# The last 64 query rows of a head pair: one unit for both batches, on four 64x64 pieces of TensorE's array

## The chip, the cores and the metric

One core of one Trainium2 chip runs the whole program. The metric is the device time of one execution in microseconds (us), as a median over several runs.

## What is computed

Attention with a learned relative bias over 2 batches, 8 heads, 576 positions and 64 dimensions, then two gated layers over its 1152 tokens (512 to 1536 to 512), the second with a norm ahead of it. The change touches the attention alone:

```python
scores = scale * np.matmul(q, k.transpose(0, 1, 3, 2))
...
scores = scores + bias.transpose(2, 0, 1)[None, :, :, :]
scores = scores - np.max(scores, axis=-1, keepdims=True)
attn = np.exp(scores)
attn = attn / (np.sum(attn, axis=-1, keepdims=True) + 1e-09)
return np.matmul(attn, v).astype(np.float32)
```

The bias depends on head and positions, not on the batch, so both batches use the same bias rows.

## The kernel before

576 query rows are four blocks of 128 and one of 64 (`it` 0 to 4; block 4 is the one of 64). Heads go in pairs (`hp` 0 to 3), since a head has 64 dimensions. A unit is a batch, a head pair and a row block: 40 units, in the order of `UNITS` (L264 to L267). The last eight, 32 to 39, are the 64-row units, for each head pair batch 0 and then batch 1.

A unit goes through these stages, in float32:

- `qk_mm` (L302): scores `s`. The stationary operand is a head's queries, 64 dimensions on the partitions, and the moving one its keys, in two chunks of 288 columns. Head 0 of the pair lies on partitions 0 to 63 of `raw`, head 1 on 64 to 127. With 128 rows each head fills a PSUM tile of two banks; with 64 rows both heads share one tile, head 0 in its partitions 0 to 63 and head 1 in 64 to 127, so that one reduction and one exponential serve both. Such a unit has one "job" where a 128-row unit has two (L298).
- `reduce_min` (VectorE, L322) adds the bias and takes the row's minimum of the negated scores; `expo` (ScalarE, L342) makes the exponentials and their sums; `normal` (L356) divides, on GpSimd but for the first units.
- `transp` (L370) transposes the probabilities in blocks of 128 columns into banks `tp`, up to four blocks a bank: nine blocks for 128 rows, five, the last of 64 columns, for 64 rows. Two or three copies (`evac`, L705 on ScalarE, L703 on VectorE) bring them to `pt`.
- `pv` (L391) multiplies with V: five steps of two matmuls, one per head, on the two column halves of the array. For 64 rows the fifth step has 64 contraction rows. `xf`, `xh`, `xl` are the copy of the result and its split into two parts for the expert layers. V has three parts in memory, `vp`: head 0, head 1 shifted by 64 rows (its first 64 positions lie alone in chunk 0), and head 1 unshifted, which only the 64-row units use and which `load_last` (L146) brings late.

The loop over `n` (L693) runs `qk_mm(n + 1)`, the reductions and exponentials of unit `n`, `normal(n - 1)`, and `transp` and `pv` of unit `n - 3`. The order of these within a pass is written out by hand (`ORDERS`, L58): one string for passes 0 to 19, one for later passes, one for the drain of the last four passes, in which no scores are left. In the drain the first two of a unit's copies go to ScalarE and the third to VectorE; in the passes before it the first goes to ScalarE and the rest to VectorE.

`C` in these strings is `advance`: one micro step of the weights' preparation for the expert layers in a pass (two and more in the drain). A weight piece of 128x512 comes from memory as pairs of words (`wr`) and is split by four micro steps on VectorE, ScalarE and GpSimd (L478 to L496) into a high and a low part, `wh` and `wl`. Behind attention come 72 steps `s` of the expert layers: `gate_val` (products `gv`, L511) and `out_mm` (products `acc`, L541), with five micro steps a step or fewer. The first `gate_val`, `gv0`, stands in the drain of attention. Micro steps go by count and by the number of pieces done, not by time.

The SyncE queue issues the loads, in program order: bias rows `bt` up to four units ahead into three buffers, V's parts, weights two pieces ahead.

## Time and profile before

| | us |
|---|---|
| median of 3 runs | 658.17 |
| lowest, highest | 657.31, 658.32 |
| span of the profiled execution | 654.7 |
| PE busy | 641.9 |
| DVE busy | 486.9 |
| ACT busy | 354.4 |
| POOL busy | 209.6 |

The page gives the profiled execution by its span, from the first to the last instruction; the median lies 3.5 us above it, which is what stands around the span. PE is TensorE, DVE VectorE, ACT ScalarE, POOL GpSimd, SPq the SyncE queue. The attention ends at about 198 us of the span, the rest is the expert layers. The start of an instruction in a timeline row is measured; its length holds its latency, so the time that a block takes on PE is read from its start to the start of the next block.

### The profile page before, as it was taken

The numbers are of one execution on the slowest core, as the hardware profiler recorded it, in microseconds if no ns is written. First come the engines' busy times: TensorE is split into PE (matmuls) and PEld (weight loads), VectorE is DVE, ScalarE is ACT, GpSimd is POOL, SyncE is SP. The second block draws the span as 40 slices with busy tenths as digits, with TensorE's granted clock in tenths as the row PEclk, the third lists the DMA queues.
The fourth block names the chain that finished last, engine by engine and source line by source line (L and its number), as shares of the span: only waits on it lengthen the run. The fifth ranks groups of instructions, "written<-read, shape, count | busy, mean of one in ns | idle before, by whom it ended". The sixth has DMA issues, their size and how long they took to land.

```text
span 654.7 us, 11794 instructions
## 1 busy us (share of the span) xinstructions
PE 641.9 (98%) x4454; PEld 576.1 (88%) x4454; DVE 486.9 (74%) x980; ACT 354.4 (54%) x753; POOL 209.6 (32%) x237
## 2 busy tenths in 40 slices
PE   8889999999999999999999999999999999999997
PEld 4336666777779999999999999999999999999997
DVE  6889898688659987888888888787877878321322
ACT  4769888888786655445444545453545535111110
POOL 6401677566454332333323321110423423000000
PEclk9979999999999999999999999999999999999999
DMA  8875855664124333433332330220324321000111
GB/s 202 278 263 185 223 173 183 220 227 121 52 65 130 111 115 97 129 97 98 102 102 90 127 95 34 65 66 32 102 93 129 97 76 55 2 0 1 49 49 48
DMA packets 28089, 71.73 MB, mean 110 GB/s; under 512 B 3457, under 2 KB 6529, under 8 KB 28033
## 3 DMA queue, kind: packets, MB, share of 16 engines
q1 hardware_dynamic: 27168, 69.80, 34.7%
q10 hardware_dynamic: 864, 1.18, 0.5%
q8 instruction: 35, 0.57, 0.4%
q14 instruction: 22, 0.17, 0.1%
HBM read 57.72 MB, written 13.25 MB: 108 GB/s over the span
## 4 chain that ended last, share of the span: by engine, by line
PE 94%; ACT 1%; issue 0%; DVE 0%; DVEq 0%
PE gv L511 46%; PE s L312 7%; PE pv L404 7%; PE tp L384 6%; PE bps L213 4%; PE acc122a L541 1%; PE acc102b L541 1%; PE acc100b L541 1%; PE acc121b L541 1%; PE acc120b L541 1%; PE acc101b L541 1%; PE acc110b L541 1%; PE acc030b L541 1%; PE acc112b L541 1%; PE acc111b L541 1%; PE acc032b L541 1%
## 5 line engine op out<-in xcount | busy, mean ns | idle before, releaser
L488 POOL TENSOR_TENSOR ff<-ff,wr 128x512 int32<-128x512 int32 x72 | 113.3, 1574 | 250.8 <-DVE ff L487 130.8
L517 DVE TENSOR_TENSOR g<-gv,sg 128x384 f32<-128x384 f32 x72 | 40.0, 556 | 95.6 <-PE gv L511 81.6
L519 ACT ACTIVATE gh<-g 128x384 fp32r<-128x384 f32 x72 | 37.8, 525 | 101.1 <-DVE g L517 101.1
L511 PE MATMUL gv<-nh,wv 128*128 128x384 f32 x288 | 76.5, 337 | 0.0
L511 PE MATMUL gv<-xh,wh 128*128 128x384 f32 x216 | 73.2, 339 | 0.0
L511 PE MATMUL gv<-xl,wh 128*128 128x384 f32 x216 | 72.9, 337 | 0.0
L511 PE MATMUL gv<-xh,wl 128*128 128x384 f32 x216 | 72.8, 337 | 0.0
L478 DVE TENSOR_SCALAR ff<-wr 128x512 uint32<-128x512 uint32 x72 | 62.1, 863 | 0.0
L515 ACT ACTIVATE sg<-gv 128x384 f32<-128x384 f32 x72 | 34.6, 481 | 50.1 <-PE gv L511 50.0
L330 DVE CUSTOM_DVE_ANT_0 t<-s,bt 128x576 f32<-128x576 f32 x72 | 51.8, 751 | 13.4 <-PE s L312 11.3
L312 PE MATMUL s<-raw 64*128 64x288 f32 (+1 forms) x320 | 52.3, 427 | 4.9 <-issue 2.9
L351 ACT ACTIVATE p<-t,mn 128x576 f32<-128x576 f32 x72 | 55.2, 767 | 3.0 <-DVE mn L330 3.0
L404 PEld LDWEIGHTS pv<-pt,v 128*64 128x64 f32 (+1 forms) x800 | 40.2, 136 | 17.2 <-ACT pt L705 11.1
L195 DVE TENSOR_SCALAR ht<-w1l,bpc 128x304 f32<-128x304 f32 (+17 forms) x100 | 53.5, 599 | 0.0
L511 PEld LDWEIGHTS gv<-nh,wv 128*128 128x128 f32 x288 | 52.4, 188 | 0.0
L404 PE MATMUL pv<-pt,v 128*64 128x128 f32 (+2 forms) x800 | 49.6, 268 | 1.4 <-ACT pt L705 1.4
L492 ACT ACTIVATE wh<-ab 128x512 fp32r<-128x512 f32 x42 | 26.4, 630 | 45.2 <-DVE ab L491 44.7
L525 DVE TENSOR_TENSOR gl<-g,gh 128x384 fp32r<-128x384 f32 x72 | 45.3, 629 | 7.0 <-ACT gh L519 7.0
L487 DVE SCALAR_TENSOR_TENSOR ff<-wr,ff 128x512 uint32<-128x512 uint32 x72 | 49.1, 682 | 0.0
L491 DVE SCALAR_TENSOR_TENSOR ab<-ab,ff 128x512 f32<-128x512 f32 x72 | 49.1, 682 | 0.0
L511 PE MATMUL gv<-nh,wh 128*128 128x384 f32 x144 | 48.7, 338 | 0.0
L366 POOL TENSOR_SCALAR p<-p,rs 128x576 f32<-128x576 f32 x60 | 48.2, 815 | 1.4 <-DVE rs L361 1.1
(358 smaller groups left out, 1583.3 us busy)
## 6 DMA issues: line engine op xcount, KB each, us to landing
wr<-wts SPq DMA_DIRECT2D x72, 512.0 KB, 3.6
bias_d<-be SPq DMA_DIRECT2D x36, 295.5 KB, 4.5
bt<-bias_d SPq DMA_DIRECT2D x16, 576.0 KB, 4.8
raw<-qk SPq DMA_DIRECT2D x16, 288.0 KB, 6.5
v<-vp SPq DMA_DIRECT2D x8, 320.0 KB, 4.5
v<-vp SPq DMA_DIRECT2D x8, 160.0 KB, 4.7
bt<-bias_d SPq DMA_DIRECT2D x8, 144.0 KB, 3.3
out<-part SPq DMA_DIRECT2D x6, 192.0 KB, 1.9
```

Source lines behind the costliest of these rows:

```text
L195: nc.vector.tensor_scalar(ht, src, bpc[:, t : t + 1], 0.0, op0=ALU.add, op1=ALU.max)
L312: nc.tensor.matmul(dst, raw[r, 0, it * 128 : it * 128 + rows_of(it)], raw[r, 1, hf * 288 : hf * 288 + 288], start=True, stop=True,)
L330: nc.vector.tensor_tensor_reduce(t, sp[:, :, :288], bt[:, j].rearrange("p (a c) -> p a c", a=2), -SCALE, 3.0e38, ALU.add, ALU.min, mn[:, j ...
L351: nc.scalar.activation(p[:, j], t.rearrange("p a c -> p (a c)"), AF.Exp, bias=mn[:, j : j + 1], scale=-1.0, accum_out=sm[:, j : j + 1],)
L366: nc.gpsimd.tensor_scalar(p[:, j], p[:, j], rs[:, j : j + 1], 1.0, op0=ALU.mult, op1=ALU.mult)
L404: nc.tensor.matmul(box["ps"][j * 64 : j * 64 + 64, :n], v[:k, 2 * j if it == 4 else j, c, :], pt[:k, c, j * 64 : j * 64 + 64] if it == 4 e ...
L478: nc.vector.tensor_scalar(ff, hw, 3, 0x3FFFFFFF, op0=ALU.logical_shift_left, op1=ALU.bitwise_and)
L487: nc.vector.scalar_tensor_tensor(ff, hw, 0xC0000000, ff, op0=ALU.bitwise_and, op1=ALU.bitwise_or)
L488: nc.gpsimd.tensor_tensor(ff.bitcast(I32), ff.bitcast(I32), lw.bitcast(I32), op=ALU.add)
L491: nc.vector.scalar_tensor_tensor(ab, ab, TINY_HI, ff.bitcast(F32), op0=ALU.is_ge, op1=ALU.mult)
L511: nc.tensor.matmul(ps[:, :CH], wt[:, cs], xt[:, cc, :], start=(k == 0), stop=(k == 11))
L541: nc.tensor.matmul(dst, st_[:, m * 128 : m * 128 + 128], mv, start=(head and k == 0), stop=(last and k == 2))
```

## The change

The 64-row units 32 to 39 become four, 32 to 35, one per head pair, with `None` for the batch. Such a unit has two jobs again, one per batch: the score tile `s{n}_0` belongs to batch 0 and `s{n}_1` to batch 1, each with head 0 in partitions 0 to 63 and head 1 in 64 to 127. So that the four products of a chunk (two batches, two heads) lie on four different pieces of the array, batch 1 keeps its heads in the other halves of `raw` (`half`). The probabilities of both batches are one row of 1152 columns and are transposed in nine blocks; block 4 holds the last 64 columns of batch 0 and the first 64 of batch 1. V for batch 1 is therefore taken shifted by 64 rows, and `load_last` puts head 0 shifted into its third part by three DMAs, where batch 0 keeps one. All products have 128 contraction rows; where a block holds columns of the other batch, V's rows are zero. Both batches' products go into one bank, side by side. The loop has 36 passes instead of 40. `BLK`, `groups_of` and `IT_OF` give the same blocks as before, and without `jobs` every unit has two reductions, exponentials and divisions; `place` is the splitting into `xh` and `xl` by itself.

```diff
@@ -129,11 +140,15 @@
 
     raws = {}
 
+    def half(b, h):
+        x = (h + b) % 2 * 64
+        return slice(x, x + 64)
+
     def load_raw(b, hp):
         t = wk.tile([128, 2, S], F32, tag=f"raw{hp // 2}", name=f"raw{b}{hp}", bufs=4)
         raws[b, hp] = t
         for h in range(2):
-            r = slice(h * 64, h * 64 + 64)
+            r = half(b, h)
             nc.sync.dma_start(t[r], qk[b, hp][:, r, h].rearrange("w p s -> p w s"))
 
     vs = {}
@@ -144,7 +159,13 @@
         nc.sync.dma_start(vs[b, hp][:, :2], vp[b, hp][:, :2])
 
     def load_last(b, hp):
-        nc.sync.dma_start(vs[b, hp][:, 2], vp[b, hp][:, 2])
+        v, src = vs[b, hp], vp[b, hp]
+        if b == 0:
+            nc.sync.dma_start(v[:, 2], src[:, 2])
+            return
+        nc.sync.dma_start(v[64:, 2], src[:64, 0])
+        nc.sync.dma_start(v[:64, 2, 1:], src[64:, 0, :4])
+        nc.sync.dma_start(v[:64, 2, 0], src[:64, 1, 0])
 
     def drain(q, k=99):
         while q and k:
@@ -263,65 +285,57 @@
 
     BLOCKS = [(hp, it) for hps in ((0, 1), (2, 3)) for it in ITS[:3] for hp in hps]
     BLOCKS += [(hp, it) for it in ITS[3:] for hp in range(NP)]
-    UNITS = [(b, hp, it) for hp, it in BLOCKS for b in range(B)]
+    UNITS = [(b, hp, it) for hp, it in BLOCKS for b in (range(B) if rows_of(it) == 128 else (None,))]
     NU = len(UNITS)
     st = {}
 
     def load_bias(n):
-        _, hp, it = UNITS[n]
+        b, hp, it = UNITS[n]
         bt = wk.tile([128, 2, S], F32, tag="bt", name=f"bt{n}", bufs=3)
 
...
-        st[n, "bt"] = st[n + 1, "bt"] = bt
-
-    ahead = list(range(0, NU, B))
+        st[n, "bt"] = bt
+        if b is not None:
+            st[n + 1, "bt"] = bt
+
+    ahead = [n for n in range(NU) if UNITS[n][0] != 1]
...
     def qk_mm(n):
         b, hp, it = UNITS[n]
-        raw = raws[b, hp]
-        sps = [bank2(f"s{n}_{j}") for j in range(jobs(n))]
-        if it == 4:
-            order = [(h, hf, sps[0][h * 64 : h * 64 + 64, hf, :288]) for h in range(2) for hf in range(2)]
+        sps = [bank2(f"s{n}_{j}") for j in range(2)]
+        if b is None:
+            plan = [(x, h, sps[x][h * 64 : h * 64 + 64]) for x in range(2) for h in range(2)]
         else:
-            order = [(h, hf, sps[h][:, hf, :288]) for hf in range(2) for h in range(2)]
-        for h, hf, dst in order:
-            r = slice(h * 64, h * 64 + 64)
-            nc.tensor.matmul(
-                dst,
-                raw[r, 0, it * 128 : it * 128 + rows_of(it)],
-                raw[r, 1, hf * 288 : hf * 288 + 288],
-                start=True,
-                stop=True,
-            )
+            plan = [(b, h, sps[h]) for h in range(2)]
+        r0, rows = BLK[it]
+        for hf in range(2):
+            cs = slice(hf * 288, hf * 288 + 288)
+            for x, h, dst in plan:
+                raw, r = raws[x, hp], half(x, h)
+                nc.tensor.matmul(dst[:, hf, :288], raw[r, 0, r0 : r0 + rows], raw[r, 1, cs], start=True, stop=True)
         for j, sp in enumerate(sps):
             st[n, "s", j] = sp
 
     def reduce_min(n, j):
-        if j >= jobs(n):
-            return
         if j == 0:
             st[n, "mn"] = w2.tile([128, 2], F32, tag="mn", name=f"mn{n}", bufs=3)
         bt, mn = st[n, "bt"], st[n, "mn"]
@@ -368,66 +379,70 @@
     pts = {}
 
     def transp(n):
-        b, hp, it = UNITS[n]
-        pt = pts[b, hp, it] = w2.tile([128, 9, 128], F32, tag="pt", name=f"pt{n}")
-        p = st.pop((n, "p"))[0]
-        p2 = p.rearrange("p a c -> p (a c)")
-        width = S if it == 4 else 2 * S
-        blocks = [p2[:, a : min(a + 128, width)] for a in range(0, width, 128)]
+        pt = pts[UNITS[n]] = w2.tile([128, 9, 128], F32, tag="pt", name=f"pt{n}")
+        p = st.pop((n, "p"))[0].rearrange("p a c -> p (a c)")
         evac = []
-        i = 0
-        while i < len(blocks):
-            m = min(4, len(blocks) - i)
+        for i in range(0, 9, 4):
+            m = min(4, 9 - i)
             tp = bank(f"tp{n}_{i}")
             for x in range(m):
-                k = blocks[i + x].shape[1]
-                nc.tensor.transpose(tp[:k, x * 128 : x * 128 + 128], blocks[i + x], ident)
-            evac.append((pt[:k, i : i + m], tp[:k, : m * 128].rearrange("p (m c) -> p m c", m=m)))
-            i += m
+                a = (i + x) * 128
+                nc.tensor.transpose(tp[:, x * 128 : x * 128 + 128], p[:, a : a + 128], ident)
+            evac.append((pt[:, i : i + m], tp[:, : m * 128].rearrange("p (m c) -> p m c", m=m)))
         return evac
 
     peq = []
...
     def pv(u):
         b, hp, it = u
         pt = pts.pop(u)
-        v = vs[b, hp]
-        n = rows_of(it)
+        r0, n = BLK[it]
         box = {}
-
-        def step(c):
+        if b is None:
+            todo = [(x, c, j) for x in range(B) for c in range(5) for j in range(2)]
+        else:
+            todo = [(b, c, j) for c in range(5) for j in range(2)]
+        k = len(todo) // 5
+
+        def one(x, c, j):
+            v = vs[x, hp]
+            if b is None:
+                at, w, m = x * 64, (2 * j if x == 0 else 2 - j), pt[:, 4 * x + c, j * 64 : j * 64 + 64]
+            else:
+                at, w, m = 0, j, pt[:, 4 * j + c]
+            dst = box["ps"][j * 64 : j * 64 + 64, at : at + n]
+            nc.tensor.matmul(dst, v[:, w, c, :], m, start=(c == 0), stop=(c == 4))
+
+        def step(i):
             def go():
-                if c == 0:
+                if i == 0:
                     box["ps"] = bank(f"pv{b}{hp}{it}")
-                for j in range(2):
-                    k = 64 if it == 4 and c == 4 else 128
-                    nc.tensor.matmul(
-                        box["ps"][j * 64 : j * 64 + 64, :n],
-                        v[:k, 2 * j if it == 4 else j, c, :],
-                        pt[:k, c, j * 64 : j * 64 + 64] if it == 4 else pt[:, j * 4 + c, :n],
-                        start=(c == 0),
-                        stop=(c == 4),
-                    )
-                if c < 4:
+                for t in todo[i * k : i * k + k]:
+                    one(*t)
+                if i < 4:
                     return
...
                 xf = w2.tile([128, 128], F32, tag="xf", name=f"xf{b}{hp}{it}")
...
+                if b is None:
+                    for x in range(B):
+                        place(xf[:, x * 64 : x * 64 + 64], x, hp, x * S + r0, n)
+                else:
+                    place(xf, b, hp, b * S + r0, n)
```

On PE, in the passes of the 64-row units: `s36` is the scores of unit 36, `tp34` the transposes of unit 34, `pv104` the products of batch 1, head pair 0, block 4. Before:

```order
L312 MATMUL s36_0_2643<-raw02_856 64x288 x4
L404 MATMUL pv133_2654<-pt31_2583,v13_1540 64x128 x10
L384 MATMUL tp33_0_2681<-ident_94,p33_2530 128x128 x4
L384 MATMUL tp33_4_2686<-ident_94,p33_2530 64x128
L312 MATMUL s37_0_2688<-raw12_912 64x288 x4
L404 MATMUL pv004_2699<-pt32_2635,v00_519 64x64 x10
L384 MATMUL tp34_0_2723<-ident_94,p34_2578 128x128 x4
L384 MATMUL tp34_4_2728<-ident_94,p34_2578 64x128
L312 MATMUL s38_0_2730<-raw03_966 64x288 x4
L404 MATMUL pv104_2741<-pt33_2680,v10_587 64x64 x10
```

and now, from the scores of the last unit, 35:

```order
L334 MATMUL s35_0_2631<-raw03_966 64x288 x2
L334 MATMUL s35_1_2632<-raw13_1039 64x288 x2
L334 MATMUL s35_0_2631<-raw03_966 64x288 x2
L334 MATMUL s35_1_2632<-raw13_1039 64x288 x2
L425 MATMUL pv033_2650<-pt30_2561,v03_1464 64x128 x10
L390 MATMUL tp32_0_2677<-ident_94,p32_2496 128x128 x4
L390 MATMUL tp32_4_2682<-ident_94,p32_2496 128x128 x4
L390 MATMUL tp32_8_2687<-ident_94,p32_2496 128x128
L425 MATMUL pv133_2698<-pt31_2618,v13_1540 64x128 x10
```

Four score matmuls in one row have become eight, which change between the batches' tiles, and the transposes of a 64-row unit are the nine of a 128-row unit.

On PE in the drain, behind `gv0`, before:

```order
L384 MATMUL tp38_0_2925<-ident_94,p38_2759 128x128 x4
L384 MATMUL tp38_4_2930<-ident_94,p38_2759 64x128
L404 MATMUL pv124_2942<-pt37_2854,v12_1392 64x64 x10
L384 MATMUL tp39_0_2960<-ident_94,p39_2801 128x128 x4
L384 MATMUL tp39_4_2965<-ident_94,p39_2801 64x128
L404 MATMUL pv034_2974<-pt38_2924,v03_1464 64x64 x10
L404 MATMUL pv134_2998<-pt39_2959,v13_1540 64x64 x10
```

and now:

```order
L390 MATMUL tp34_0_2821<-ident_94,p34_2613 128x128 x4
L390 MATMUL tp34_4_2826<-ident_94,p34_2613 128x128 x4
L390 MATMUL tp34_8_2831<-ident_94,p34_2613 128x128
L425 MATMUL pvNone14_2844<-pt33_2731,v01_661 64x64 x10
L425 MATMUL pvNone14_2844<-pt33_2731,v11_733 64x64 x10
L390 MATMUL tp35_0_2874<-ident_94,p35_2670 128x128 x4
L390 MATMUL tp35_4_2879<-ident_94,p35_2670 128x128 x4
L390 MATMUL tp35_8_2884<-ident_94,p35_2670 128x128
L425 MATMUL pvNone24_2894<-pt34_2820,v02_1322 64x64 x10
L425 MATMUL pvNone24_2894<-pt34_2820,v12_1392 64x64 x10
L425 MATMUL pvNone34_2930<-pt35_2873,v03_1464 64x64 x10
L425 MATMUL pvNone34_2930<-pt35_2873,v13_1540 64x64 x10
```

The same four blocks of products and transposes in turn, each for two batches: the transposes of two units and the products of three.

On ACT in the drain, behind the copy `gh` of the first expert step, where `pt` are the copies of transposed blocks and `ab`, `wr`, `wh` micro steps of weights. Before:

```order
L519 ACTIVATE gh0_2922<-g32_0_2920 128x384
L705 ACTIVATE pt38_2924<-tp38_0_2925 128x512
L480 ACTIVATE ab6_2938<-wr6_2632 128x512
L481 ACTIVATE wr6_2632<-wr6_2632 128x512
L705 ACTIVATE pt38_2924<-tp38_4_2930 64x128
L416 ACTIVATE xf124_2953<-pv124_2942 128x64
L422 ACTIVATE xh2_119<-xf124_2953 128x64
L492 ACTIVATE wh5_1792<-ab5_2869 128x512
L705 ACTIVATE pt39_2959<-tp39_0_2960 128x512
L705 ACTIVATE pt39_2959<-tp39_4_2965 64x128
```

and now:

```order
L534 ACTIVATE gh0_2818<-g32_0_2816 128x384
L720 ACTIVATE pt34_2820<-tp34_0_2821 128x512
L495 ACTIVATE ab5_2840<-wr5_2438 128x512
L496 ACTIVATE wr5_2438<-wr5_2438 128x512
L720 ACTIVATE pt34_2820<-tp34_4_2826 128x512
L436 ACTIVATE xfNone14_2865<-pvNone14_2844 128x128
L403 ACTIVATE xh1_118<-xfNone14_2865 128x64
L403 ACTIVATE xh2_119<-xfNone14_2865 128x64
L507 ACTIVATE wh4_1790<-ab4_2753 128x512
L720 ACTIVATE pt35_2873<-tp35_0_2874 128x512
L720 ACTIVATE pt35_2873<-tp35_4_2879 128x512
```

The second copy of a unit has grown from 64x128 to 128x512 and stands, as before, behind two micro steps; the pieces that are being prepared at this place are one number lower.

## Rows read from the trace of the kernel before

**Rows 1.** The page: span, and PE's busy time with its share and instructions.
```profile
span 654.7 us, 11794 instructions
PE 641.9 (98%) x4454; PEld 576.1 (88%) x4454; DVE 486.9 (74%) x980; ACT 354.4 (54%) x753; POOL 209.6 (32%) x237
```
**Rows 2.** Stretches: length, then busy time (instructions) of each engine, PEclk, DMA share, GB/s.
```profile
60.00:160.00 100.00, 100.00 (x1060) 71.39 (x1054) 83.16 (x230) 85.90 (x218) 64.21 (x102) 1.00 0.63 191
157.53:161.08 3.55, 3.55 (x39) 2.73 (x38) 3.18 (x9) 2.59 (x8) 3.16 (x5) 1.00 0.23 81
161.08:164.58 3.50, 3.50 (x39) 2.53 (x38) 2.55 (x10) 2.59 (x8) 1.93 (x4) 1.00 0.50 159
172.70:198.00 25.30, 23.92 (x299) 18.25 (x297) 15.46 (x41) 19.81 (x52) 13.26 (x20) 1.00 0.21 64
198.00:300.00 102.00, 102.00 (x586) 101.84 (x584) 89.82 (x139) 54.88 (x106) 34.93 (x23) 1.00 0.37 114
```
**Rows 3.** Timeline of PE: start, length, instruction, [idle before <-releaser].
```profile
158.70 1.31 PE L404 MATMUL pv<-pt,v 128*64 128x128 f32 x20
159.94 1.20 PE L384 MATMUL tp<-ident,p 128*128 128x128 f32 x9
161.08 1.19 PE L312 MATMUL s<-raw 64*64 64x288 f32 x8
...
179.71 0.77 PE L384 MATMUL tp<-ident,p 128*128 128x128 f32 x5
180.40 1.20 PE L312 MATMUL s<-raw 64*64 64x288 f32 x8
181.52 0.95 PE L404 MATMUL pv<-pt,v 128*64 128x64 f32 x20
182.40 0.77 PE L384 MATMUL tp<-ident,p 128*128 128x128 f32 x5
...
192.51 0.71 PE L384 MATMUL tp<-ident,p 128*128 128x128 f32 x5
...
195.72 0.95 PE L404 MATMUL pv<-pt,v 128*64 128x64 f32 x20 [0.93 <-ACT pt L705]
197.11 0.95 PE L404 MATMUL pv<-pt,v 128*64 128x64 f32 x20 [0.45 <-ACT pt L705]
197.99 0.45 PE L511 MATMUL gv<-xh,wh 128*128 128x384 f32 x1
```
**Rows 4.** Timeline of PE in slices: 180.39 to 180.45, to 180.75, 157.52 to .55, 178.82 to .86, 107.04 to .08.
```profile
180.40 0.47 PE L312 MATMUL s<-raw 64*64 64x288 f32 x2
180.40 0.71 PE L312 MATMUL s<-raw 64*64 64x288 f32 x4
157.53 0.51 PE L312 MATMUL s<-raw 64*128 64x288 f32 x2
178.83 0.28 PE L404 MATMUL pv<-pt,v 128*64 128x64 f32 x2
107.05 0.44 PE L213 MATMUL bps<-ht,prms 128*32 128x272 f32 x4
```
**Rows 5.** Timeline of PE in two slices, 178.92 to 178.95 and 178.92 to 179.30.
```profile
178.83 0.34 PE L404 MATMUL pv<-pt,v 128*64 128x64 f32 x4
178.83 0.69 PE L404 MATMUL pv<-pt,v 128*64 128x64 f32 x16
```
**Rows 6.** Timeline of ACT in the drain of attention.
```profile
193.80 0.58 ACT L705 ACTIVATE pt<-tp 128x512 f32<-128x512 f32 x1
194.28 0.67 ACT L480 ACTIVATE ab<-wr 128x512 f32<-128x512 f32 x1
194.85 0.66 ACT L481 ACTIVATE wr<-wr 128x512 int32<-128x512 uint32 x1
```
**Rows 7.** Timeline of the SyncE queue: issuing V's third parts of two units.
```profile
147.26 1.06 SPq L147 DMA_DIRECT2D v<-vp  x2
```
**Rows 8.** The page's groups: one of DVE's four steps on a weight piece.
```profile
L487 DVE SCALAR_TENSOR_TENSOR ff<-wr,ff 128x512 uint32<-128x512 uint32 x72 | 49.1, 682 | 0.0
```

More of the change, by code (lines that the diff above doesn't have):

```diff
@@ L64, with groups_of @@
 TINY_HI = 1.125 * 2.0**-15
+BLK = ((0, 128), (128, 128), (256, 128), (384, 128), (512, 64))
 def rows_of(it):
-    return 128 if it < 4 else 64
+    return BLK[it][1]
+def groups_of(it):
+    a, r = BLK[it]
+    return range(a // 16, (a + r) // 16)
+IT_OF = {T: it for it in range(5) for T in groups_of(it)}
 def bias_width(it):
@@ L239, in bias_end @@
             nc.gpsimd.tensor_scalar(dst, src, 1.0, 1.0, op0=ALU.mult, op1=ALU.mult)
-        a = (T // 8) * 128 + rows_of(T // 8) - 1 - right
-        r = (T % 8) * 128
-        nc.sync.dma_start(bias_d[T // 8][r : r + 128, a : a + S + 15], be)
+        it = IT_OF[T]
+        a = sum(BLK[it]) - 1 - right
+        r = (T - groups_of(it)[0]) * 128
+        nc.sync.dma_start(bias_d[it][r : r + 128, a : a + S + 15], be)
         stored.append(T)
-    GORDER = [T for it in ITS for T in range(8 * it, min(8 * it + 8, 36))]
+    GORDER = [T for it in ITS for T in groups_of(it)]
     GORDER = GORDER[2:8] + GORDER[:2] + GORDER[8:]
@@ L276, in load_bias @@
         flat = bias_d[it].rearrange("a w -> (a w)")
-        for h in range(2 if it == 4 else 1):
+        for h in range(2 if b is None else 1):
             o = r - 1 + (2 * hp + h) * w
             rows = flat[o : o + r * (H * w - 1)].rearrange("(i k) -> i k", k=H * w - 1)
-            if it == 4:
+            if b is None:
                 nc.sync.dma_start(bt[h * 64 : h * 64 + 64, 0], rows[:, :S])
@@ L332, in reduce_min @@
             sp[:, :, :288],
-            bt[:, j].rearrange("p (a c) -> p a c", a=2),
+            bt[:, 0 if UNITS[n][0] is None else j].rearrange("p (a c) -> p a c", a=2),
             -SCALE,
@@ L357, in normal @@
         p, sm = st[n, "p"]
-        k = jobs(n)
-        nc.vector.tensor_scalar(sm[:, :k], sm[:, :k], 1e-9, None, op0=ALU.add)
+        nc.vector.tensor_scalar(sm, sm, 1e-9, None, op0=ALU.add)
         rs = w2.tile([128, 2], F32, tag="rs", name=f"rs{n}", bufs=3)
-        nc.vector.reciprocal(rs[:, :k], sm[:, :k])
-        for j in range(k):
+        nc.vector.reciprocal(rs, sm)
+        for j in range(2):
             if n in NORM_DVE:
@@ L370, in transp, with place @@
     def transp(n):
-        b, hp, it = UNITS[n]
-        pt = pts[b, hp, it] = w2.tile([128, 9, 128], F32, tag="pt", name=f"pt{n}")
-        p = st.pop((n, "p"))[0]
-        p2 = p.rearrange("p a c -> p (a c)")
-        width = S if it == 4 else 2 * S
-        blocks = [p2[:, a : min(a + 128, width)] for a in range(0, width, 128)]
+        pt = pts[UNITS[n]] = w2.tile([128, 9, 128], F32, tag="pt", name=f"pt{n}")
+        p = st.pop((n, "p"))[0].rearrange("p a c -> p (a c)")
         evac = []
-        i = 0
-        while i < len(blocks):
-            m = min(4, len(blocks) - i)
+        for i in range(0, 9, 4):
+            m = min(4, 9 - i)
             tp = bank(f"tp{n}_{i}")
             for x in range(m):
-                k = blocks[i + x].shape[1]
-                nc.tensor.transpose(tp[:k, x * 128 : x * 128 + 128], blocks[i + x], ident)
-            evac.append((pt[:k, i : i + m], tp[:k, : m * 128].rearrange("p (m c) -> p m c", m=m)))
-            i += m
+                a = (i + x) * 128
+                nc.tensor.transpose(tp[:, x * 128 : x * 128 + 128], p[:, a : a + 128], ident)
+            evac.append((pt[:, i : i + m], tp[:, : m * 128].rearrange("p (m c) -> p m c", m=m)))
         return evac
     peq = []
+    def place(ps, b, hp, lo, n):
+        a = lo
+        while a < lo + n:
+            e = min(lo + n, (a // CH + 1) * CH)
+            d = slice(a % CH, a % CH + e - a)
+            src = ps[:, a - lo : e - lo]
+            nc.scalar.activation(xh[a // CH][:, hp, d], src, AF.Copy)
+            nc.gpsimd.tensor_tensor(xl[a // CH][:, hp, d], src, xh[a // CH][:, hp, d].bitcast(F32), op=ALU.subtract)
+            a = e
     def pv(u):
@@ L428, in step @@
+                if b is None:
+                    for x in range(B):
+                        place(xf[:, x * 64 : x * 64 + 64], x, hp, x * S + r0, n)
+                else:
+                    place(xf, b, hp, b * S + r0, n)
             return go
-        peq.extend(step(c) for c in range(5))
+        peq.extend(step(i) for i in range(5))
     def members(l, g):
```

21 lines of the change are left out of this document (2 added, 19 removed).

## Prediction, made before the changed kernel ran

> **What bounds the kernel now.** I read the page first: TensorE (PE) is busy 98% of the span of 654.7 us [rows 1]. Then the stretches: from 60 to 160 us and from 198 to 300 us PE has no idle time at all, at clock 1.00 (2.4 GHz), while VectorE (DVE), the next busiest, is at 83 to 88%. Only the end of attention, 172.70 to 198.00, has a gap, 23.92 us busy of 25.30 [rows 2]. So in attention a microsecond of PE time is a microsecond of the result, and the expert layers behind it, which start when attention's last product is done, should move as a block. The reader is to see in [rows 3] that PE runs three blocks per loop pass back to back: scores (`s`), products with V (`pv`) of the unit four before, transposes (`tp`) of the unit three before, all as if nothing else existed.
>
> **The cycle of a 64-row unit, before.** Starts in [rows 3]: transposes 179.71 to 180.40, 0.69; scores 180.40 to 181.52, 1.12; products 181.52 to 182.40, 0.88. That is 2.69 us, and eight such units (two batches, four head pairs) exist. A 128-row unit takes 1.14 for its nine transposes (159.94 to 161.08) and 1.24 for its products, and its whole pass lasts 3.55 [rows 2, 3]. The 64-row unit has half the rows and yet costs three quarters.
>
> **Scores: the main term.** The program has four score matmuls per 64-row unit, the trace has eight records (x8), so each float32 matmul is two passes. They start in pairs: in a slice of 0.06 us at 180.40 two stand, and by 180.75 four [rows 4]. A pass of 288 columns thus runs on two pieces of the array at a time, and four starts fill the 1.12 us. The new unit has eight matmuls, sixteen passes, on four pieces: row half x column half. If all four run together, sixteen passes are again four starts and 1.12 us for both batches; the price of the second unit, 1.12, is gone, four times: **4.49 us**. No row shows four pieces of 64x64 at once, so this is the one unknown price. From both sides: four at once gives 4 x 1.12 less; two at once gives no saving; one at a time gives 16 passes of 0.24 us (1.12 less the ends, by four starts), 3.9 us against 2.25, a loss of 1.6 per head pair. I take four, because each kind of neighbour is seen running together: different row halves into different banks (64x128 scores, two records in 0.03 us at 157.53), different column strips on the same rows with different moving data (`pv`, two at 178.83; `bps`, four strips at 107.05), and row half plus column half crossed (64x64 scores) [rows 4].
>
> The first two matmuls of the new order are the two heads of batch 0: different row halves, different column halves, the same bank of scores. In the rows of before the two records that start together at 180.40 must be just that pair, since the two column chunks of one head use the same piece and each head begins with the same chunk, that is the same bank. The Trainium skill says against it ("TensorEngine Tiling (Array Packing)", Restrictions and Gotchas) that different row tiles cannot access the same PSUM bank simultaneously; by that rule at most two pieces would run here, the scores would save nothing, and the sum below would be 3.5 instead of 7.8 us. The paired starts of the 64x64 scores speak against the rule as it is written, at least where the rows go to different partitions of the bank.
>
> **Transposes.** Before, each unit has 576 columns in five blocks, the last of 64; both together ten. Now the 1152 columns of both batches are one row of nine full blocks, and the middle one holds the end of batch 0 and the start of batch 1. 2 x 0.69 becomes 1.14: 0.24 per pair, **1.0 us** in all.
>
> **Products.** The number stays, 20 per head pair, all 64 columns wide, in column pairs. Before, each unit has eight pairs of passes with 128 rows, then two with 64 rows, and the start of a block and the change to 64 rows cost time: 0.88 per unit. Between the end of the second pair and of the eighth lie 0.35 us [rows 5], 0.058 a pair. Twenty pairs without a change of shape: the eighth ends 0.69 after the start, twelve more add 0.70, 1.39; in the 128-row block the next block begins 0.07 before the last end (1.31 long, next start 1.24 later [rows 3]), so 1.32. Against 1.76: 0.44, four times **1.76 us**. The zero rows that V is padded with replace the 64-row passes.
>
> Sum of PE work: 4.49 + 1.0 + 1.76 = **7.25 us**.
>
> **The gap at the end.** Before, PE stands 0.93 and 0.45 us before the last two product blocks, both for ScalarE's (ACT) copies of transposed blocks [rows 3]. In the drain the first expert product `gv0` runs on PE until G = 192.51, and behind it ACT does the copy of 512 columns, two weight steps, the second copy, and so on [rows 3, 6]. Now three whole units are left instead of three half ones: the second copy has 512 columns too, 0.58 long, instead of 128, but PE has 1.32 instead of 0.88 of products per unit as cover. ACT starts the first copy at G+1.29; the copy and the two steps take 0.48 + 0.57 + 0.56 from start to start, then a copy of 0.5, G+3.4. PE does nine transposes and the products of unit 33 until G+2.46, the first four transposes of unit 35 until 2.9, then needs a bank that the second copy frees (four banks go round): 3.45, a stall of 0.5. The products of unit 34 end near 5.5; ACT by then has the output copies (0.6 by my estimate, three of 128 partitions and at most 128 columns), one weight step (0.5) and two copies of 512 (1.0), 5.5 to 5.7: a stall of 0.1 to 0.2. So I take **0.7 of gap instead of 1.38**; ends: none, and 2.5 if one more of ACT's or DVE's steps comes late (0.5 to 0.7 each, two or three of them).
>
> **Costed at nothing.** The second score reduction, exponential and normalization per pass: a merged pass has on DVE, ACT and GpSimd what a 128-row pass has, and there DVE is busy 3.18 of 3.55 us with PE never idle; merged passes have 3.50 on PE (as 161.08 to 164.58, where DVE does 2.55 now) [rows 2]. That cover is thin, 0.3 us: three passes without it would cost 1 us. The eight extra DMAs for V on the SyncE queue: about 0.5 us each to issue (1.06 for two [rows 7]), 4 us spread over eight passes of 3.5, and V's third part is used some 20 us after its load. Bias loads: the same eight transfers, but they now follow a pass apart and wait for one of three buffers, so the queue holds back the weight loads behind it by a pass, 3.5 us; weights are fetched two pieces ahead, some eight passes. The four weight steps that lose their pass: attention has 36 passes instead of 40 and each carries one step, so the pipeline of split weights is one piece behind at the same place in the program. A piece costs DVE four steps of about 0.68, 2.7 us, and from 198 to 300 DVE has 12 us free [rows 2, 8]. The first weights that could be late are piece 4's, for the second half of `gv1`: their last step, `wl4`, follows on DVE the copy of unit 35's last block (near G+4.5) and one weight step, and waits for ACT's `wh4` (near G+4.6), so it ends near G+5.8, while the second half of `gv1` begins 2.1 us after G+7. If that cover fails, a piece is 2.7 us.
>
> **Sum.** 7.25 + 0.7 = 7.95; for four starts instead of two in each round, some 0.02 us, I take off 0.1: **7.8 us**, span 654.7 to 646.9. The runs' median is 658.17, 3.5 us above the profiled span; that stays: **650.4 us**.
>
> **Rivals.**
> *Two pieces at a time* (by the bank or the shared row strip): scores save nothing, 7.95 - 4.49 = 3.5, 654.7 us. For it: no row with four; against: all pairs seen. 9%.
> *The drain or the late weights eat two to three microseconds:* a whole piece, 2.7 us late before `gv1` or the output product, 650.4 + 2.7 = 653.1, or the gap at its upper end, 652.0. For it: ACT already ended both waits [rows 3, 6]. 6%.
> *One piece at a time* (the other side): if a piece must wait for the one before, since consecutive matmuls share alternately bank and rows, a merged unit's scores take 3.9 instead of 2.25 us, 6.6 lost against 3.4 won elsewhere: 661.4. It decides once the scores take over 3.1 us per unit, on average 1.25 pieces at a time. Against it stand the pairs of [rows 4]. 3%.
> *It moves nothing:* the split weights come at a pace of their own, and the expert layers wait for what attention has won, 657.3 to 658.3 as now. For it: the steps are a piece behind; against: from 198 to 300 the DMA engines are at 0.37 of their time and DVE has room [rows 2]. 2%.
>
> **How the numbers follow.** Forecast, four pieces and a short gap: 80%, with 649.5 (no gap) less 0.5 for the spread of runs (657.31 to 658.32) down to 649.0, and 652.0 up with the long gap. The range takes in the late weights with the spread: 649.0 to 653.2, leaving out two at a time, one at a time and no change, 14%. About 0.2%, 1.3 us, is what a measurement tells here from no change. Faster by more: 80 + 9 + 6, less one for cases in between, 94%; within: 2%; slower: 4%.
>
> **What would show it.** Scores of a merged unit: sixteen records, four starting within some 0.05 us, 1.12 to 1.15 us before the next block (2.2 would be two at a time, over 3 one). Nine transposes in 1.14, twenty product pairs in 1.32. `gv1` starts near 190.1 instead of 197.99, with PE waits of 0.2 to 1.2 us for ACT's copies in the drain; behind it PE without gaps, ending the same distance later. I am wrong if a merged pass on PE exceeds 3.6 us, if `gv1` waits for a weight, or if a stretch in the expert layers shows idle PE.

## The result, and the profile after

The change takes 650.93 us (median of 4 runs, 650.60 to 651.69) against 658.25 for the kernel before in the same series (4 runs): ratio 0.9885 with the interval 0.9869 to 0.9902. The forecast was 650.4 us, in a range from 649.0 to 653.2.

The profiled execution has a span of 649.9 us and a time of 651.69; PE's busy time went from 641.9 [rows 1] to 637.6. The page of the change:

```profile
span 649.9 us, 11776 instructions
PE 637.6 (98%) x4450; PEld 575.7 (89%) x4450; DVE 487.3 (75%) x972; ACT 352.6 (54%) x745; POOL 210.5 (32%) x237
```

PE's timeline of the change, a merged pass, the first drain block and the end of attention (the rows that answer to [rows 3]):

```profile
164.49 1.20 PE L334 MATMUL s<-raw 64*64 64x288 f32 x16
165.62 1.31 PE L425 MATMUL pv<-pt,v 128*64 128x128 f32 x20
166.86 1.20 PE L390 MATMUL tp<-ident,p 128*128 128x128 f32 x9
168.00 1.20 PE L334 MATMUL s<-raw 64*64 64x288 f32 x16
...
179.79 1.17 PE L390 MATMUL tp<-ident,p 128*128 128x128 f32 x9
180.90 1.39 PE L425 MATMUL pvNone<-pt,v 128*64 128x64 f32 x40
182.21 0.44 PE L526 MATMUL gv<-xh,wh 128*128 128x384 f32 x1
...
188.87 1.52 PE L390 MATMUL tp<-ident,p 128*128 128x128 f32 x9
190.31 2.75 PE L425 MATMUL pvNone<-pt,v 128*64 128x64 f32 x80
193.00 0.44 PE L526 MATMUL gv<-xh,wh 128*128 128x384 f32 x1
```

Sixteen score passes now take 1.13 us from start to the next block's start (164.49 to 165.62); eight took 1.12 [rows 3]. Two short slices of the same timeline, up to 164.55 and up to 164.85, show four starts and then eight, where [rows 4] show two and four:

```profile
164.49 0.47 PE L334 MATMUL s<-raw 64*64 64x288 f32 x4
164.49 0.72 PE L334 MATMUL s<-raw 64*64 64x288 f32 x8
```

The stretches of the change (columns as in [rows 2]):

```profile
20.00:48.00 28.00, 22.21 (x153) 9.06 (x154) 21.15 (x53) 16.65 (x37) 5.75 (x12) 0.76 0.73 243
164.49:168.00 3.51, 3.51 (x47) 2.56 (x46) 3.16 (x12) 2.59 (x8) 1.92 (x4) 1.00 0.83 230
193.00:300.00 107.00, 107.00 (x615) 106.70 (x612) 94.87 (x145) 58.82 (x113) 38.76 (x28) 1.00 0.37 112
```

A merged pass lasts 3.51 us with DVE at 3.16 and PE never idle, and behind the second expert product `gv1` the view has no idle time of PE up to 300 us. I cut both traces at the first 64-row scores and at `gv1`. Before, 161.08 to 197.99 is 36.91 us; after, 164.49 to 193.00 is 28.51: **8.40 us won in this stretch**. From `gv1` to the end it is 456.73 (to 654.71) and 456.86 (to 649.86). But the 64-row scores begin 3.41 us later than before, though of what the change touches only loads and the halves of `raw` have run by then. The first stretch above shows a difference: granted clock 0.76 there, while the same stretch of the kernel before has 0.88:

```profile
20.00:48.00 28.00, 22.80 (x165) 9.59 (x159) 23.96 (x62) 18.93 (x41) 5.74 (x12) 0.88 0.76 253
```

With two levels, 1.2 and 2.4 GHz, a mean of 0.76 over 28 us is 13.4 us at the lower one, and 0.88 is 6.7. Half of the difference is 3.4, an upper estimate of what it costs, since PE also stands idle in this stretch.

### The profile page after: what moved, and what is told of

Its sections match the earlier page's. It is cut to its first block, busy times and chain, and to the rows that moved or that the text cites. A ratio compares the mean times of both kernels' runs of the same rounds, so it can differ in the third digit from the quotient of the medians.

```text
span 649.9 us, 11776 instructions
## 1 busy us (share of the span) xinstructions
PE 637.6 (98%) x4450; PEld 575.7 (89%) x4450; DVE 487.3 (75%) x972; ACT 352.6 (54%) x745; POOL 210.5 (32%) x237
## 4 chain that ended last, share of the span: by engine, by line
PE 93%; DVE 1%; issue 1%; ACT 0%; DVEq 0%
PE gv L526 47%; PE s L334 7%; PE pv L425 6%; PE tp L390 6%; PE bps L234 3%; PE acc122a L556 1%; PE acc102b L556 1%; PE acc100b L556 1%; PE acc121b L556 1%; PE acc101b L556 1%; PE acc120b L556 1%; PE acc030b L556 1%; PE acc032b L556 1%; PE acc112b L556 1%; PE acc111b L556 1%; PE acc110b L556 1%
## 5 line engine op out<-in xcount | busy, mean ns | idle before, releaser
L334 PE MATMUL s<-raw 64*128 64x288 f32 (+1 forms) x320 | 49.7, 439 | 5.7 <-issue 3.2
L526 PE MATMUL gv<-nl,wh 128*128 128x384 f32 x144 | 48.6, 337 | 0.0
L526 PE MATMUL gv<-nh,wl 128*128 128x384 f32 x144 | 48.6, 337 | 0.0
```

The lines of the kernel that those rows point to most:

```text
L334: nc.tensor.matmul(dst[:, hf, :288], raw[r, 0, r0 : r0 + rows], raw[r, 1, cs], start=True, stop=True)
L526: nc.tensor.matmul(ps[:, :CH], wt[:, cs], xt[:, cc, :], start=(k == 0), stop=(k == 11))
```

## The experiments

Each ratio is against the kernel before, run on the same chip between the runs of the experiment. "The stretch" is from the first 64-row scores to `gv1`, 28.51 us in the change and 36.91 before. "The rest" is from `gv1` to the end.

**The change again**, nothing edited.

> The changed kernel once more, beside the kernel before in the same rounds, with span and granted clock of every run. If the 0.6 us that the median fell short of the trace's gain (8.3 us from the first 64-row scores to the end) come from the clock at the start of the program, the runs of this kernel spread by 1 us or more with their clock, as those of the kernel before do, and the difference at equal clock is 7.8 to 8.4 us. If the change itself slows the first 160 us, its clock is lower in most runs than that of the kernel before, or its span longer at the same clock, and the difference stays at 7.3.

650.83 us (6 runs, 649.23 to 652.92), 0.9903 (0.9875 to 0.9930). Stretch 28.49, rest 456.85, as in the first profile; the clock from 20 to 48 us was 0.88 this time and the 64-row scores begin at 162.03, not 164.49. So 2.46 of the 3.41 us go with the clock; the other 0.95, at the same 0.88 as before, do not, and stay without an explanation here. The runs spread with their clock (0.995 to 0.987) as expected, but the expectation isn't settled: the medians differ by 7.3 us, and runs of equal mean clock by 6.7 (at 0.994) to 8.0 us (at 0.992).

**Two pieces instead of four:** batch 1 keeps its heads in the same halves as batch 0, all else stays merged.

```diff
-        x = (h + b) % 2 * 64
+        x = h * 64
```

> Batch 1 keeps its heads in the same halves as batch 0, so that of the four products of a chunk two share a piece of the array; all else as in the change. If the gain on the scores is four pieces at once, a merged unit's scores take 2.1 to 2.2 us instead of 1.13 and the time rises by 4 x 1.0 = 4.0 to 4.4 us over the changed kernel, to about 655. If the gain comes from there being half as many units and passes, the scores change little and the time stays within 1 us of the changed kernel. If a shared piece stops the queue for the others as well, scores over 2.5 us and a time over 656.5.

653.75 us (10 runs, 649.68 to 656.06), 0.9934 (0.9907 to 0.9960): 2.9 us above the change by the medians, where 4.0 to 4.4 were expected. The stretch in the trace tells more, since it lies behind the start and its clock. PE's timeline, and its slice up to 0.06 us behind the start:

```profile
163.97 2.16 PE L334 MATMUL s<-raw 64*64 64x288 f32 x16
166.06 1.31 PE L425 MATMUL pv<-pt,v 128*64 128x128 f32 x20
...
163.97 0.46 PE L334 MATMUL s<-raw 64*64 64x288 f32 x2
```

Two starts instead of four, 2.09 us instead of 1.13 for the same sixteen passes, and a stretch of 32.31: 3.80 more, four times 0.95. So close to half of the 8.40, 3.80, hangs on the four pieces; the other 4.60 come from the merging alone.

**The other order within a merged unit:** each piece's two column chunks follow each other in the program, where the change has the four pieces of one chunk and then those of the other.

```diff
-        for hf in range(2):
...
-            for x, h, dst in plan:
+        seq = [(hf, t) for t in plan for hf in range(2)] if b is None else [(hf, t) for hf in range(2) for t in plan]
+        for hf, (x, h, dst) in seq:
```

> In a merged unit the two column chunks of one piece follow each other in the program, so that consecutive matmuls stand on the same piece; in the change they go round the four pieces. If each piece takes its own next pass without waiting for the program's order, the scores stay four starts, 1.13 to 1.2 us, and the time from the first 64-row scores to the second expert product stays at 28.5 us. If passes start in the program's order, a piece's second chunk holds the next piece back, the scores take 1.8 to 2.5 us and that time is 31 to 34.

One run, 650.3 us, stretch 28.57. Four records still start within 0.06 us and the block takes 1.15:

```profile
163.07 0.49 PE L334 MATMUL s<-raw 64*64 64x288 f32 x4
...
163.07 1.22 PE L334 MATMUL s<-raw 64*64 64x288 f32 x16
164.22 1.31 PE L425 MATMUL pv<-pt,v 128*64 128x128 f32 x20
```

The pieces need not be named in turn: here a matmul for a free piece did not wait behind one for a busy piece. The kernel before shows the same with two pieces, since it names both chunks of head 0 ahead of head 1's (the order over `h` and `hf` in the diff) and its scores start in pairs [rows 4].

**64 rows where V is padded:** batch 0's fifth step uses 64 contraction rows again.

```diff
+                rows = slice(0, 64) if x == 0 and c == 4 else slice(0, 128)
...
+                rows = slice(0, 128)
...
-            nc.tensor.matmul(dst, v[:, w, c, :], m, start=(c == 0), stop=(c == 4))
+            nc.tensor.matmul(dst, v[rows, w, c, :], m[rows], start=(c == 0), stop=(c == 4))
```

> The last product pair of batch 0 in a merged unit has 64 contraction rows again, as before the change, instead of 128 with zeros; the result is the same. If the change of shape costs what the trace of before shows (a pair after it at 0.15 and 0.11 us where others take 0.058), the block of products grows from 1.32 to 1.5 to 1.6 us and the time by 0.7 to 1.1 us over the changed kernel. If the saving in the products comes only from starting a block once instead of twice, nothing moves, within 0.3 us.

651.62 us (4 runs), 0.9907 (0.9873 to 0.9940); by the medians not to be told from the change. In PE's timeline:

```profile
187.04 1.68 PE L427 MATMUL pvNone<-pt,v 128*64 128x64 f32 x40
188.65 1.20 PE L390 MATMUL tp<-ident,p 128*128 128x128 f32 x9
189.78 3.14 PE L427 MATMUL pvNone<-pt,v 128*64 128x64 f32 x80
```

A block of products that stands alone takes 1.61 us instead of 1.31 or 1.32: the two changes of shape cost 0.29. The stretch grows by only 0.67, not 4 x 0.29: the last two blocks together grow by 0.37 (3.06 against 2.69), and the wait in the transposes of unit 35 (1.44 from 188.87 to 190.31 in the change, 1.13 here) is covered by the longer products.

**Second copy of a drain unit on DVE** instead of ACT.

```diff
-        on_dve = (2,) if n < NBIAS or n >= NU else (1, 2)
+        on_dve = (2,) if n < NBIAS else (1, 2)
```

> In the drain the second copy of a unit goes to VectorE, as in the passes before, instead of behind two weight steps on ScalarE. If that copy is what PE waits for in the drain, the last transposes shrink from 1.44 to 1.13 us to the next block and the gain is 0.2 to 0.4 us. If VectorE becomes late instead (its copy stands behind the weight steps of the pass), the products wait longer by 0.3 to 1 us and the first weights of the next expert step with them.

651.01 us (6 runs), 0.9906 (0.9880 to 0.9932); stretch 28.74. ACT's wait is gone and DVE's comes in its place:

```profile
191.59 0.92 PE L425 MATMUL pvNone<-pt,v 128*64 128x64 f32 x24 [0.41 <-DVE pt L718]
```

**Second copy ahead of the weight step** in the drain's order.

```diff
-    "M0 T X0 E2 N Q E0 M1 C X1 E1 B L P0 P1 V",
+    "M0 T X0 E2 N Q E0 M1 E1 C X1 B L P0 P1 V",
```

> In the drain ScalarE does the second copy of a unit right behind the first, ahead of the weight steps. If PE's last stall comes from that copy standing behind two weight steps, the 1.44 us of the last transposes shrink to 1.13 and the stretch from the first 64-row scores to the second expert product from 28.5 to 28.2 us. If the stall comes from elsewhere (the output copies, a bank), nothing moves. If the weight steps were the tighter wait, a later wait of PE for weights appears and takes the gain back.

650.94 us (4 runs), 0.9880 (0.9851 to 0.9908); stretch 28.56, no gain. The transposes no longer wait, but the products of units 34 and 35 now do, by 0.19 and 0.12 us. The order of ACT's work moves the wait; the whole of it stays.

**Weight step last in the drain's order.**

```diff
-    "M0 T X0 E2 N Q E0 M1 C X1 E1 B L P0 P1 V",
+    "M0 T X0 E2 N Q E0 M1 X1 E1 B L P0 P1 C V",
```

> In the drain the weight steps stand behind the output copies too. If what is left of the gap there is ScalarE's whole queue ahead of the output copy that frees the next products' bank, the stretch from the first 64-row scores to the second expert product falls from 28.5 to 28.2 us. If the weights, later by about half a microsecond, are the next wait, PE's wait at the first output product of the second token chunk, 21 us behind the second expert product, grows from 0.1 to 0.4 us or more.

One run, 652.12 us. The stretch is 28.82, 0.3 longer where 0.3 shorter was expected, and the rest 457.60. The waits of PE in this trace (what waits, for what: total us, count, longest):

```profile
PE acc001a L556 <- ACT part L568: 0.7, 1, 0.7
PE pvNone L425 <- ACT pt L720: 0.6, 1, 0.6
```

The second is in the drain. The first is the wait of 0.1 us that the expectation names, grown to 0.7 as it says for weights that come later: the first output product of the second group of tokens waits until ACT has copied the partial sums `part` out of its bank.

**Four weight steps fewer:** the last four passes with scores carry none, so the split weights come one piece later again.

```diff
-            "C": lambda: n >= NBIAS + LAG and advance(...),
+            "C": lambda: n >= NBIAS + LAG and not NU - 4 <= n < NU and advance(...),
```

> The last four passes of attention carry no weight step, so the split weights are two pieces behind the kernel before, not one. This measures the cover that the prediction claimed for the lost steps. If the margin is the 3 us estimated for piece 4, the second expert product starts as in the change (28.5 us after the first 64-row scores) and its second half or the products behind it stand for at most 0.5 us. If the margin was thin, PE shows waits for the weights of piece 3 or 4 of 1 to 3 us, and the end moves by as much. If the weights limit the whole expert part, the stretch from the second expert product to the end, 456.9 us, grows by 2 us or more.

One run, 654.07 us. The stretch is the change's, 28.51, and the second expert product runs through without a wait; the rest is 461.36, 4.5 longer, nearly all of it at the same place. PE's timeline:

```profile
212.17 0.34 PE L526 MATMUL gv<-xh,wl 128*128 128x384 f32 x1
215.25 0.45 PE L556 MATMUL acc001a<-gh,wh 128*128 128x384 f32 x1 [2.74 <-ACT part L568]
...
217.99 0.52 PE L526 MATMUL gv<-xh,wh 128*128 128x384 f32 x1
218.31 0.52 PE L526 MATMUL gv<-xl,wh 128*128 128x384 f32 x1
```

A stop of 2.74 us, and behind it matmuls of the same shape 0.32 us apart (217.99 to 218.31), where they are 0.17 to 0.18 apart at full clock, which costs another 1.7 us; those two make the 4.5. In the change's second profile the same place reads on PE

```profile
211.57 0.34 PE L526 MATMUL gv<-xh,wl 128*128 128x384 f32 x1
211.86 0.44 PE L556 MATMUL acc001a<-gh,wh 128*128 128x384 f32 x1
212.13 0.34 PE L556 MATMUL acc001a<-gl,wh 128*128 128x384 f32 x1
```

and on ACT

```profile
208.88 0.64 ACT L507 ACTIVATE wh<-ab 128x512 fp32r<-128x512 f32 x1 [2.07 <-DVE ab L506]
...
210.95 0.85 ACT L568 ACTIVATE part<-acc000a 128x384 f32<-128x384 f32 x2
```

0.29 us between the starts 211.57 and 211.86 where 0.17 is the pitch: ACT's copy ends at 211.80 and PE has waited 0.1 us for it. The copy stands on ACT behind a weight step, `wh`, for which ACT itself has waited 2.07 us, for DVE's step `ab`; so both queues are in this chain. In the kernel before the same two rows read

```profile
218.31 0.85 ACT L553 ACTIVATE part<-acc000a 128x384 f32<-128x384 f32 x2
...
219.04 0.34 PE L511 MATMUL gv<-xh,wl 128*128 128x384 f32 x1
219.21 0.44 PE L541 MATMUL acc001a<-gh,wh 128*128 128x384 f32 x1
```

The pitch holds, 0.17, but the copy ends at 219.16, only 0.05 us ahead. So the cover at this place, which the prediction did not look at, was thin before the change and is gone after it.

**Two weight steps a pass** in the last four passes with scores, to give the steps back.

```diff
-            "C": lambda: n >= NBIAS + LAG and advance(EARLY if live else EARLY + MORE, 1 if live else 2),
+            "C": lambda: n >= NBIAS + LAG and advance(EARLY if live else EARLY + MORE, 2 if n >= NU - 4 else 1),
```

> The changed kernel with two weight steps instead of one in each of the last four passes of attention, so that the split weights are as far as in the kernel before. If VectorE's cover in a merged pass is as thin as 0.3 us, the passes lengthen by 0.2 to 0.5 us each and the stretch from the first 64-row scores to the second expert product from 28.5 to 29.3 to 30.5 us, while the 0.1 us wait of PE 21 us behind the second expert product goes. If the other engines have room enough, that stretch stays at 28.5 and only the 0.1 us goes.

One run, 656.63 us; stretch 32.01, 3.5 longer. The merged passes with scores keep 3.50 to 3.51, but in the first passes without scores PE waits for copies on ACT and DVE:

```profile
181.60 0.63 PE L390 MATMUL tp<-ident,p 128*128 128x128 f32 x4 [0.36 <-ACT pt L720]
183.51 0.74 PE L390 MATMUL tp<-ident,p 128*128 128x128 f32 x5 [1.28 <-DVE pt L718]
```

and from 184.4 to 187.8 the granted clock is 0.50, that is 1.2 GHz, 1.7 us lost besides. 0.36 + 1.28 + 1.7 is 3.3 of the 3.5. The wait ahead of `acc001a` did not go either:

```profile
218.75 0.34 PE L526 MATMUL gv<-xh,wl 128*128 128x384 f32 x1
219.19 0.44 PE L556 MATMUL acc001a<-gh,wh 128*128 128x384 f32 x1
```

By the pitch it is 0.26 us, and `acc001a` starts 21.32 us behind `gv1`, as in the change (21.34 and 21.36), not 21.22 as before. So it isn't shown that the first 0.1 us there come from the four lost steps; that later weight steps make it longer is shown by the two runs above.

**Matmuls on constants in the first waits.** The runs of one kernel differ by several us, their mean clock differs with them, and in the profiles the clock from 20 to 48 us does too; this fills the waits there, ahead of the scores of four units with 12 matmuls each, or of three units with 6, in the change, and the latter in the kernel before too (`FILL` is 12 or 6). The waits in PE's timeline of the change, some of those it fills:

```profile
29.59 2.35 PE L334 MATMUL s<-raw 64*128 64x288 f32 x8 [1.94 <-DVE mn L344]
35.49 2.93 PE L334 MATMUL s<-raw 64*128 64x288 f32 x8 [1.48 <-issue]
43.54 2.58 PE L334 MATMUL s<-raw 64*128 64x288 f32 x8 [1.75 <-issue]
```

```diff
+    def fill(n):
+        if n < 4:
+            idle = bank(f"fill{n}")
+            for _ in range(FILL):
+                nc.tensor.matmul(idle[:, :128], ones, ones, start=True, stop=True)
...
-            "Q": lambda: n + 1 < NU and qk_mm(n + 1),
+            "Q": lambda: n + 1 < NU and (fill(n), qk_mm(n + 1)),
```

Of twelve in the change:

> Twelve matmuls on constants, into a bank nobody reads, stand ahead of the scores of units 1 to 4, where PE waits 1.4 to 2 us in the first 50 us of the program; the change is otherwise as it is. If the spread of the runs (648 to 653 us) is the half clock that falls into that stretch, it does not fall any more, the first 64-row scores start near 159 us instead of 162 to 164.5, all runs lie within 1 us of each other and the median drops by 3 to 4 us. If VectorE sets that stretch anyway, the clock stays up and the time does not move. If the filling delays the scores, the first 64-row scores start later by up to 4 x 1.3 us.

Of six in the change:

> The change with six filling matmuls ahead of the scores of units 1 to 3, 1.45 us each at full clock where twelve took 2.9 and PE's waits there are 1.4 to 2 us. If the clock stays up with these too, the first 64-row scores start near 159 us, where twelve put them at 161.5, and the median falls from 649.1 to 646.0 to 647.0. If six are too few, the half clock comes back in some runs, and the runs spread again to 651.

Of six in the kernel before:

> The kernel before the change with the same filling, so that the change can be measured without the clock's chance at the start. If the traces' account is whole, this kernel takes 8.2 to 8.5 us more than the change with the same filling (36.9 against 28.5 us from the first 64-row scores to the second expert product, 456.7 against 456.85 behind it), near 654.5 to 655. If the change also costs something in the first 160 us, the difference is 7.3 us or less.

Twelve: 649.09 us (6 runs, 648.65 to 649.45), 0.9850 (0.9826 to 0.9875). Six: 648.44 us (5 runs, 647.00 to 648.92), 0.9841 (0.9823 to 0.9858), the lowest median here, though the two intervals overlap and 646.0 to 647.0 was expected. Six in the kernel before: 655.13 us (6 runs), 0.9945 (0.9930 to 0.9960). The early stretch with six in the change:

```profile
20.00:48.00 28.00, 26.42 (x209) 14.12 (x212) 25.30 (x67) 20.07 (x43) 5.88 (x12) 1.00 0.82 270
```

Clock 1.00 where the change's own two profiles have 0.76 and 0.88. In PE's timeline there, one filling and the scores behind it:

```profile
27.28 1.60 PE L713 MATMUL fill<-ones 128*128 128x128 f32 x12
...
29.79 1.91 PE L335 MATMUL s<-raw 64*128 64x288 f32 x8 [0.91 <-DMA bt<-bias_d]
```

Here the filling of 1.60 us ends ahead of what the scores wait for, and costs nothing; twelve matmuls take 2.94, longer than the waits they fill (1.48 to 1.94 us above), and the 64-row scores begin at 161.46 instead of 159.76, so of the expectation for twelve the runs within 1 us came true, and the start near 159 and the 3 to 4 us did not. Filled, both kernels reach those scores at the same time, 159.59 before and 159.76 after, and stretch and rest are 36.90 and 458.15 before, 28.56 and 456.82 after: with the clock at 1.00 up to there the change costs nothing ahead of its own stretch, 0.17 us in these two traces. The difference of the two medians, 6.7, is less than expected, and by its number alone it falls to the expectation's other branch (7.3 or less), which these starts speak against: four of the five runs with filling in the change had a mean clock of 0.996 or 0.997 over the program, and two of the six of before. At equal clock the spans differ by 8.1 (653.2 and 645.1 at 1.000) and about 7.8 (654.3 to 654.6 and 646.2 to 647.1). Where in the four runs of the change the lower clock lies isn't shown, as the one trace is of the run at 1.000; in the trace of before it lies in the drain (last section). So it stays open why the medians' difference falls short of the traces' gain, by about 1 us without filling and by 1.5 us or more with it.

## Why the prediction was right, and where it was off

**Scores: right.** 4.49 us were forecast; eight blocks of 1.12 became four of 1.13, 4.45. The unknown price, four 64x64 pieces at once, is shown by the slices and by the run with two pieces (+3.80). The Trainium skill ("TensorEngine Tiling (Array Packing)", Restrictions and Gotchas) has it that different row tiles cannot access the same PSUM bank simultaneously. The traces don't agree where the tiles go to different partitions: batch 0's two heads lie in different row halves and share a bank of scores, batch 1's share another, and four records start in 0.06 us. Different row tiles into one bank and the same partitions were not tried.

**Transposes and products: right.** 1.0 and 1.76 were forecast. The undisturbed transposes of a merged unit take 1.07 to 1.13, together 1.1 less than before. The products take 1.31 to 1.32, as worked out, 1.73 less in all. That a change of shape within a block costs time is shown by the run that puts one back, there and back, 0.29 for a merged unit.

**The gap: right wait, too large.** 1.38 was to become 0.7; by the pitch of the blocks it became 0.36 (PE's view shows 28.41 us busy of the 28.51, since its lengths hold latency). The wait named, unit 35's transposes for the bank that ACT's second copy frees, is there, with 0.3 (188.87 to 190.31 is 1.44 against 1.13) instead of 0.5; of the 0.1 to 0.2 for the products some 0.05 is left. ACT's second copy, and the weight load (PEld) of unit 35's last transpose:

```profile
189.41 0.59 ACT L720 ACTIVATE pt<-tp 128x512 f32<-128x512 f32 x1
...
190.05 0.14 PEld L390 LDWEIGHTS tp<-ident,p 128*128 128x128 f32 x1 [0.33 <-ACT pt L720]
```

The copy ends at 190.00, 3.52 us behind the end of `gv0` at 186.48, nearly as forecast (3.45). What was mis-sized is PE's work ahead of the wait: eight transposes of unit 35 and not four. The three terms and the gap, 4.45 + 1.1 + 1.73 + 1.02, are 8.3 of the 8.40. The three runs that move the copy, or the weight step behind which it stands, moved the wait and made the stretch no shorter. So no single place in ACT's order sets the gap; that ACT's queue as a whole does is argued, not shown, and with the copy on DVE the wait was for DVE.

**"Costed at nothing": held in the time, but not by the cover that I worked out.** DVE's thin cover in a merged pass held (3.51, never idle). For the four weight steps I named `wl4` as the first that could be late, with 3 us in hand. No weight of `gv1` came late, even with a piece less. The runs show another place as the tight one: `acc001a`, 21.35 us behind `gv1`, which waits for ACT's `part` copies. There the cover was 0.05 us before the change; now PE waits 0.1 us, and one more piece costs 4.5 us. The step that failed is the choice of one weight's readiness as the test; the queues of ACT and DVE, in which weight steps and copies stand behind one another, had to be followed as well. That the cost stayed at 0.1 us was luck. The rival "late weights" was nearer than its 6% say.

**From span to median: the term of the sum that was wrong.** I carried 3.5 us from the profiled span to the median, as what stands around the span. In the runs that list both, time and span lie 1.7 to 2.0 us apart (651.69 and 649.9 for the change). The rest of the 3.5 was the run: the profiled execution of before had a mean clock of 0.994, above that of most of its runs. Seventeen runs of the kernel before in the first series go from 654.0 us at a mean clock of 1.000 to 660.3 at 0.987. So the forecast's nearness to the median, 0.5 us, is partly luck, two errors that met: the gain by the traces behind the first 64-row scores is 8.40 - 0.13 = 8.27, more than the 7.8 forecast, and that by the medians, 658.25 to 650.93, is 7.3, less. The two profiles of the change show what the clock at the start does, 2.46 us between 0.76 and 0.88; how often it falls lower in one kernel than in the other isn't settled by these few runs. It also moved `gv1`, which was to start near 190.1: it starts at 193.00 in the first profile and at 190.52 in the second.

## What to carry to other kernels

Where products leave part of the array empty, look for independent ones that fill the other pieces: the price of a block was here the longest piece's, in both orders in which the program named them. Before counting a shorter stage as won, follow every queue that its passes fed, since work counted by passes comes later in the program, and see how much cover each reader has: at the tight one it was 0.05 us before the change, and none after it. A comparison of two profiles should be cut at milestones, since what stands ahead of the change can differ by more than a third of its gain.

## What was not expected of the hardware

In this dense program the clock fell behind short stops, and the fall could cost more than the stop. Behind a stop of 1.28 us in one run and one of 2.74 us in another PE ran at 1.2 GHz for a while, at 1.7 us lost each; so it did behind the two waits of the drain in the filled kernel before, whose rest is 1.4 us longer than in the plain one (458.15 against 456.73), with a clock of 0.83 around `gv1`, from 193 to 203 us:

```profile
193.00:203.00 10.00, 8.63 (x71) 8.04 (x70) 8.78 (x13) 7.92 (x20) 4.79 (x6) 0.83 0.39 106
```

The plain kernel before has the same two waits, 0.93 and 0.45 us [rows 3], and no fall behind them (1.00 in [rows 2]): the same stops are punished in one execution and not in another. Early in the program it is waits of 1.5 to 1.9 us that go with the lower clock, and six matmuls without use in each bring 3.8 us in the kernel before (658.93 to 655.13 in one series) and 2.4 in the change (650.83 to 648.44, medians of two series), a third to a half of what the change itself brings. The Trainium skill ("TensorE: Matmul & The Clock Gate", Part 1) says that the number of slow matmuls at a kernel's start differs from run to run. No trace here shows that of the first matmuls, since from 0 to 20 us the granted clock is 1.00 in both profiles of the change; what differs from run to run here lies behind the waits, 0.76 and 0.88 from 20 to 48 us.
